# A gated recurrence and a highway layer: one product for e in most units, another order of the work, y in two tiles

## The chip, the cores and the metric

One core of a Trainium2 chip runs the whole kernel. The metric is the device time of one execution in microseconds, as the median of several runs. The profile shows one execution; its span, from the first to the last instruction, is shorter than the time of a run, which has some work around it.

## What is computed

x and f_logit have 4 sequences of 6336 steps with 256 channels each, in float32.

```python
sig = 1.0 / (1.0 + np.exp(-f_logit))
f = lower_bound[None, None, :] + (1.0 - lower_bound[None, None, :]) * sig
i = 1.0 - f
for t in range(S):
    h = f[:, t] * h + i[:, t] * x[:, t]
    y[:, t] = h
...
H = np.maximum(x @ w_h, 0.0)
T = 1.0 / (1.0 + np.exp(-(x @ w_t + b_t)))
return (T * H + (1.0 - T) * x).astype(np.float32)
```

In the last three lines, x is the y of the recurrence, as 25344 tokens of 256 channels.

## The kernel before, in words

The tokens are cut into 28 **units** (`parts`, line 42): units 0, 1 and 27 have 2 blocks of 128 tokens, units 2 and 26 have 4, all the others 8. The 256 channels are two halves of 128, so that in the middle of the kernel a channel lies on a partition and the tokens along the free dimension. Each unit goes through the same steps; a token of the list such as `s12.1:0` names the step, the unit, the half (or piece) and the buffer slot, and a `v` at its end gives the step to VectorE:

- **l**, **x**: loads of f_logit and x (SP's queue, line 244); 1 MB each for a unit of 8 blocks.
- **u** = sigmoid(-l) on ScalarE (line 256). **b** = u * x in pieces (line 264), on GpSimd or VectorE: for a unit of 8 blocks there are two pieces of 1024 elements a partition, b.0 and b.1, for the small units one or two of 512.
- **i**: PE transposes u half by half (line 271); **f** = 1 - c u from PSUM (lines 280 and 282), on ScalarE or VectorE. **p**: PE transposes pairs of b (line 291); it needs all pieces of b of its unit.
- **s**: the recurrence as one scan for each half (line 308) on VectorE, cut where a sequence begins; it reads f and the transposed b and writes y in bfloat16. A unit's scan starts from the last column of the scan before it, so the scans of a half form a chain.
- **z**, **g**: the two matrix products on PE (lines 320 and 114); **t** = sigmoid(z) on ScalarE (line 333); **d** = max(ncc y, g) on VectorE (line 337), where the weights have been changed so that this is relu less y in scaled form.
- **e**: d = d * t (line 343), on GpSimd or VectorE, in the pieces that the last entry of `units` gives (line 45).
- **o**: PE adds y and e and transposes them back (lines 365 and 366); **c** copies PSUM to SBUF (line 376 on VectorE, line 378 on ScalarE); **w** stores (line 382, SP's queue). o of a piece needs the e of its columns in both halves.
- **k** and `*n` put idle matmuls on PE (lines 125 and 114). Some tokens without a number are preparations: cc, dg, WT, WH, cb, pc, pb, and wt, wh for the weights' loads.

What sets the order: the list `order` (lines 48 to 98) is written out and read from its start to its end, and `tc.keep_in_program_order` keeps every engine's and every DMA queue's instructions in that order. So a step that waits holds everything behind it on its engine. Slots name buffers: a step that writes a slot waits until the readers of the slot's last contents are through. The waits between engines are put in by the tile framework.

One wait is put in by hand: `shared` (line 178). After VectorE has a product of two operands (b or e; also the preparations), the next such product on GpSimd in the list waits for it (only the next one, since the record is removed then). Nothing makes a product on VectorE wait for GpSimd. One line says it:

```python
tc.add_manual_dep(ins.ins, held.pop().ins.name, ...
```

y, d and t are each one tile for both halves of a unit (`flat`, line 296; `half` cuts the columns of one half out of it). y has four slots, d and t three each.

Of the kernel before, what the change touches and what calls it, by code (L numbers as in the profile page):

```python
# [12 lines left out]
BF16 = mybir.dt.bfloat16  # L13
# [6 lines left out]
def kernel(  # L20
# [53 lines left out]
p15.1:1 s15.1 c12.1:1 b17.1:2 f16.0:2 z14.1:0 z14.0:2 p16.0:0 s16.0:1 c12.0:3 t14.1:1 t14.0 g14.0:1 d14.0 i16.1:1
w11.1 l19:1 u18:3 x18:0 b17.0 e14.0 g15.1:0 d15.1:2 z15.0:2 i17.1:0 x19:3 f16.1:0 b18.0:3 p16.1:1 f17.1:1 b18.1 l20:2
s16.1 o13.1:1 t15.0:0 p17.0:0 g15.0:0 w12.1 d15.0 c13.1:0 u19:1 b19.1:1 o13.0:2 p17.1:1 z15.1:1 c13.0:2 z16.0:0
s17.1:2 t15.1 t16.0:1 z16.1:2 s17.0 g16.0:1 w13.1 t16.1 i18.0:1 d16.0:0 g16.1:0 o14.0:2 i18.1:0 f18.0:0 d16.1 e15.0v
o14.1:1 p18.0:1 s18.0:3 u20:2 w12.0 z17.0:0 c14.0:0 c14.1:1 f18.1:1 g17.0:2 d17.0:1 z17.1:1 b19.0 t17.0:0 i19.1:0
# [10 lines left out]
b25.1 p24.0:0 c20.1:1 d22.0 z23.0:0 s24.0:1 g23.0:1 t23.0:2 e22.0 l26:0 o21.0:2 c21.0:2 o21.1:0 s24.1 i25.1:0 g23.1:2
c21.1:3 x26:1 e22.2 g24.1:0 d23.0:1 f25.1:1 u26:2 b26.0:1 i27.1:1 i25.0:0 f27.1:0 d23.1 w20.0 z23.1:1 p25.0:1 f25.0:2  # L90
d24.1:2 s25.0:2 z24.0:2 p25.1:0 b26.1 t23.1 o22.0:0 e23.1 o22.1:1 t24.0:0 e23.2 z24.1:2 c22.0:0 s25.1 w20.1 g24.0:0
d24.0 e23.0v w21.0 c22.1:1 t24.1 w21.1 e24.0 w22.0 i26.0:1 e24.1 z25.0:1 i27.0:0 f26.0:2 g25.0:2 e24.2 i26.1:1 d25.0:0
f27.0:1 t25.0:1 p26.0:0 f26.1:3 o23.0:0 g25.1:1 z25.1:2 p26.1:1 s26.0:3 d25.1 c23.0:0 s26.1 w22.1 o23.1:0 p27.0:0
t25.1 w23.0 c23.1:1 o24.0:1 e25.0v o24.3:2 s27.0:0 g26.0:a1 o24.2:0 c24.0:2 o24.1:1 d26.0:1 c24.3:0 c24.2 c24.1
p27.1:0 e25.1 e25.2v z26.0:2 o25.0:0 o25.1:1 z26.1:a1 s27.1 g26.1:a0 t26.0:0 z27.0:2 c25.0:3 t26.1 c25.1v o25.2:0
t27.0:1 o25.3:1 d26.1 g27.0:a0 w23.1 z27.1:a1 w24.1 w24.0 e26.0 c25.2:0 e26.1v o26.0:2 o26.1:0 d27.0:0 g27.1:a0 d27.1
w25.0 c25.3 t27.1 e27.0 e27.1v o27.0:1 c27.0v:1 c26.0:2 o27.1:a0 c26.1 w25.1 w26.0 w27.0 c27.1:3 w27.1
"""

    NU = len(units)  # L100
# [7 lines left out]
    def sb(shape, dtype, name, slot=0):  # L108
        return pool.tile(shape, dtype, tag=f"{name}{slot}", name=name)
# [56 lines left out]
    def tokens(n):  # L166
        return units[n][0] * P
# [128 lines left out]
    def flat(n, key, name, slot):  # L296
        if key not in st[n]:
            st[n][key] = sb([P, NH * NB * P], BF16, name, slot)
        return st[n][key]

    def half(n, key, h):
        return st[n][key][:, h * tokens(n):(h + 1) * tokens(n)]

    def do_s(n, h, eng, slot):
        flat(n, "y", "y", slot)
        y = half(n, "y", h)
        for fresh, c, e in pieces(n):
            pin(nc.vector.tensor_tensor_scan(y[:, c:e], st[n]["f", h][:, c:e], st[n]["bT", h][:, c:e],  # L308
                                             0.0 if fresh else carry[h], op0=ALU.mult, op1=ALU.add))
            carry[h] = y[:, e - 1:e]  # L310
# [32 lines left out]
        shared(pin(e.tensor_mul(st[n]["d"][:, a:c], st[n]["d"][:, a:c], st[n]["t"][:, a:c])), not eng)  # L343
# [79 lines left out]
```

## Time and profile before

| | |
|---|---|
| median of 3 runs | 207.93 us (207.89 to 208.76) |
| span of the profiled execution | 206.1 us |
| instructions | 4635 |
| bytes moved | 78.68 MB, mean 382 GB/s |
| mean granted TensorE clock | 0.995 |

How to read it: PE is TensorE, PEld its weight loads, DVE VectorE, ACT ScalarE, POOL GpSimd, SP the queue that issues the DMAs. A row of a group gives line, engine, operation, what it writes from what it reads, the shape, the count, busy microseconds, the mean of one in nanoseconds, and the idle time just ahead of them with what ended it. A row of the timeline begins with start and duration in microseconds and may merge several instructions that follow each other (x2 and so on). Neighbours on an engine overlap a little, so that start to start is some 0.06 us less than the mean.

### The profile page before, as it was taken

How to read it: one execution, taken by the hardware profiler on the slowest of the kernel's cores; microseconds unless marked ns; L12 is line 12 of the kernel's file. 1: busy time of each engine (PE TensorE's matmuls, PEld its weight loads, DVE VectorE, ACT ScalarE, POOL GpSimd, SP SyncE). 2: the span in 40 equal slices, each digit the busy share in tenths (PEclk: the TensorE clock that was granted, in tenths of full speed). 3: DMA queues.
4: the chain of work that ended last, by engine and by line, in shares of the span. 5: the costliest groups of instructions: out<-in, count | busy, mean ns of one | idle time of the engine just before them, and what ended most of it. 6: DMA issues, size and time to landing. Idle time of an engine off the chain costs nothing.

```text
span 206.1 us, 4635 instructions
## 1 busy us (share of the span) xinstructions
PE 192.6 (93%) x1837; PEld 133.8 (65%) x1837; DVE 194.5 (94%) x159; ACT 191.9 (93%) x192; POOL 173.8 (84%) x93
## 2 busy tenths in 40 slices
PE   7798799799998999999999999999999999999991
PEld 2366465566685776676577576677758758776770
DVE  0899999999999999999899999999999999999972
ACT  4369999999999999999999999999999999999891
POOL 3036989789979997999999999799899999998840
PEclk9999999999999999999999999999999999999997
DMA  6999999999999999999999999999999999725396
GB/s 196 370 424 422 411 418 423 409 423 417 414 423 408 429 417 426 423 420 413 425 424 416 433 411 417 429 415 418 407 422 422 414 392 378 286 104 204 138 382 248
DMA packets 16125, 78.68 MB, mean 382 GB/s; under 512 B 1764, under 2 KB 2536, under 8 KB 10216
## 3 DMA queue, kind: packets, MB, share of 16 engines
q1 hardware_dynamic: 16096, 78.39, 93.6%
q8 instruction: 14, 0.23, 0.4%
q14 instruction: 7, 0.06, 0.1%
q10 hardware_dynamic: 8, 0.00, 0.0%
HBM read 52.43 MB, written 25.95 MB: 380 GB/s over the span
## 4 chain that ended last, share of the span: by engine, by line
PE 53%; ACT 14%; DMA 13%; DVE 10%; issue 6%; POOL 2%; SPq 1%; ACTq 0%; DVEq 0%; POOLq 0%
DMA x<-in_x_dram 9%; DVE y L308 8%; PE op L366 7%; PE bT L291 7%; PE op L365 7%; PE g L320 7%; PE z L320 6%; PE uT L271 6%; PE g L114 6%; PE z L114 6%; ACT o L378 4%; ACT f L282 4%; DMA out_dram<-o 4%; ACT t L333 3%; POOL bv L264 2%
## 5 line engine op out<-in xcount | busy, mean ns | idle before, releaser
L264 POOL TENSOR_TENSOR bv<-u,x 128x1024 bf16<-128x1024 f16 (+1 forms) x49 | 100.9, 2085 | 16.9 <-DVE bt L207 10.7
L308 DVE TENSOR_TENSOR_SCAN y<-f,y,bT 128x1024 bf16<-128x1024 f16 (+5 forms) x54 | 106.8, 1989 | 0.2 <-PE bT L291 0.2
L343 POOL TENSOR_TENSOR d<-d,t 128x512 bf16<-128x512 bf16 (+3 forms) x33 | 73.3, 2234 | 9.6 <-DVE d L343 4.2
L337 DVE SCALAR_TENSOR_TENSOR d<-y,ncc,g 128x1024 bf16<-128x1024 bf16 (+2 forms) x56 | 63.1, 1137 | 1.5 <-PE g L320 1.0
L333 ACT ACTIVATE t<-z,bt 128x1024 bf16<-128x1024 f32 (+2 forms) x56 | 58.9, 1088 | 1.3 <-PE z L114 0.7
L282 ACT ACTIVATE f<-uT,ncc 128x1024 f16<-128x1024 f16 (+2 forms) x51 | 55.4, 1098 | 3.4 <-PE uT L271 2.2
L378 ACT COPY o<-op 128x1024 f32<-128x1024 f32 (+2 forms) x55 | 52.1, 984 | 2.4 <-PE op L366 1.6
L256 ACT ACTIVATE u<-l 128x2048 f16<-128x2048 f32 (+2 forms) x28 | 49.8, 1781 | 2.8 <-DMA l<-in_f_logit_dram 2.7
L366 PE MATMUL op<-ident_b,d 128*128 128x128 bf16 x396 | 49.5, 219 | 0.6 <-DVE d L343 0.6
L365 PE MATMUL op<-diag,y 128*128 128x128 f16 x396 | 49.7, 219 | 0.1
L366 PEld LDWEIGHTS <-d 128*128 128x128 bf16 x396 | 44.0, 113 | 3.2 <-DVE d L343 0.7
L365 PEld LDWEIGHTS <-y 128*128 128x128 bf16 x396 | 44.2, 113 | 1.7
L320 PE MATMUL g<-y,w_sb 128*128 128x512 bf16 (+1 forms) x112 | 39.5, 367 | 0.9 <-DVE d L337 0.7
L320 PE MATMUL z<-y,w_sb 128*128 128x512 bf16 (+1 forms) x112 | 39.3, 367 | 0.4 <-ACT o L378 0.4
L291 PE MATMUL bT<-ident_f,bv 128*128 128x128 f32 x198 | 31.8, 277 | 4.3 <-DVE y L308 2.6
L114 PE MATMUL z<-y,w_sb 128*128 128x512 bf16 x92 | 34.9, 379 | 0.0
L114 PE MATMUL g<-y,w_sb 128*128 128x512 bf16 x92 | 34.9, 379 | 0.0
L320 PEld LDWEIGHTS <-w_sb 128*128 128x128 f16 x224 | 21.6, 98 | 17.5 <-issue 0.9
L271 PEld LDWEIGHTS <-u 128*128 128x128 f16 x396 | 26.3, 98 | 10.2 <-issue 2.6
L271 PE MATMUL uT<-ident_h,u 128*128 128x128 f16 x396 | 31.2, 220 | 1.6 <-DVE y L308 0.8
L291 PEld LDWEIGHTS bT<-ident_f,bv 128*128 128x128 f32 x198 | 22.4, 141 | 12.3 <-ACT f L282 3.0
L114 PEld LDWEIGHTS <-w_sb 128*128 128x128 f16 x184 | 18.0, 98 | 16.7 <-issue 1.8
(39 smaller groups left out, 58.7 us busy)
## 6 DMA issues: line engine op xcount, KB each, us to landing
out_dram<-o SPq DMA_DIRECT2D x48, 512.0 KB, 7.7
l<-in_f_logit_dram SPq DMA_DIRECT2D x23, 1024.0 KB, 12.0
x<-in_x_dram SPq DMA_DIRECT2D x23, 1024.0 KB, 13.4
l<-in_f_logit_dram SPq DMA_DIRECT2D x2, 512.0 KB, 7.5
x<-in_x_dram SPq DMA_DIRECT2D x2, 512.0 KB, 7.2
l<-in_f_logit_dram SPq DMA_DIRECT2D x3, 256.0 KB, 2.9
x<-in_x_dram SPq DMA_DIRECT2D x3, 256.0 KB, 3.9
out_dram<-o SPq DMA_DIRECT2D x2, 256.0 KB, 16.3
```

The lines of the kernel that those rows point to most:

```text
L114: return pe.add_instruction(mybir.InstMatmult(name=nc.get_next_instruction_name(), start_tensor_calc=start, stop_tensor_calc=stop, tile_si ...
L264: shared(pin(e.tensor_mul(st[n]["bv"][:, a:c].rearrange("p k d j -> p k j d"), st[n]["u"][:, 2 * a:2 * c].rearrange("p (k j) d -> p k j d" ...
L271: pin(nc.tensor.transpose(uT[:, j * P:(j + 1) * P], st[n]["u"][:, j, h * P:(h + 1) * P], ident_h))
L282: pin(nc.scalar.activation(to, of, AF.Identity, scale=ncc[:, h:h + 1], bias=1.0))
L291: pin(nc.tensor.transpose(words[:, k:k + g * (P - 1) + 1:g], pair, ident_f))
L308: pin(nc.vector.tensor_tensor_scan(y[:, c:e], st[n]["f", h][:, c:e], st[n]["bT", h][:, c:e], 0.0 if fresh else carry[h], op0=ALU.mult, op1 ...
L320: pin(nc.tensor.matmul(p[:, a:e], w, half(n, "y", ki)[:, a:e], start=ki == 0, stop=ki == NH - 1))
L333: pin(nc.scalar.activation(half(n, "t", m), st[n]["z", m][:, :tokens(n)], AF.Sigmoid, bias=bt[:, m:m + 1]))
L337: pin(nc.vector.scalar_tensor_tensor(half(n, "d", m), half(n, "y", m), ncc[:, m:m + 1], st[n]["g", m][:, :tokens(n)], op0=ALU.mult, op1=AL ...
L343: shared(pin(e.tensor_mul(st[n]["d"][:, a:c], st[n]["d"][:, a:c], st[n]["t"][:, a:c])), not eng)
L365: pin(nc.tensor.matmul(o, half(n, "y", h)[:, cols], diag[:, h], start=True, stop=False))
L366: pin(nc.tensor.matmul(o, half(n, "d", h)[:, cols], ident_b, start=False, stop=True))
```

## The change

Three things. The pieces of e: one product of 2048 elements a partition for units 3 to 25 (so far for units 7 to 21, the others of 8 blocks in three pieces of 1024, 512 and 512). y: a tile for each half, with eight slots of half the size, where there were four slots of a whole one; `half` takes the half's tile. The list: a new one, all of it in another order. The rest are other spellings of the same code.

On VectorE's queue the new list has b0, b1, b2.1, b2.0 and b26.0 (512 each) and b3.1, b4.1 (1024 each); before it was b0, b1, b2.1 and b3.1. Its e are now e0.0, e2.1, e6, e9, e15, e17, e25 and e27.1. It has copies c24.1, c25.3 and c26.0, where there were c25.1 and c27.0, and f1.0, f9.0, f10.0 and f18.0, where there were f0.0, f1.1, f9.0, f14.0 and f22.0. On SP's queue the loads of unit 0 stand first, wt is the third, and l27 and x27 stand in the middle of the queue instead of near its start. d24.1 stands behind the scan s25.0 instead of ahead of it. The diff, with the two lists cut to the lines that matter most:

```diff
     parts = [2] * 2 + [4] + [8] * 23 + [4] + [2]
+    bcuts = {2: (0, 1), 4: (0, 1, 2), 8: (0, 2, 4)}
+    ecuts = {2: (0, 256, 512), 4: (0, 512, 1024), 8: (0, 1024, 1536, 2048)}
     units, at = [], 0
     for n, nb in enumerate(parts):
-        units.append((nb, at, {2: (0, 1), 4: (0, 1, 2), 8: (0, 2, 4)}[nb], (0, 2048) if 7 <= n <= 21 else {2: (0, 256, 512), 4: (0, 512, 1024), 8: (0, 1024, 1536, 2048)}[nb]))
+        units.append((nb, at, bcuts[nb], (0, 2048) if 3 <= n <= 25 else ecuts[nb]))
         at += nb * P
...
-l1:0 l0:1 x0:0 x1:1 k*3:a0 l2:2 wt wh x2:2 l3:3 x3:3 l4:4 pc:0 x4:4 u0:0 l27:1 l5:5 b0.0v:0 x27:0 x5:5 u1:1 cc l6:0
...
-e8.0 t10.1:2 e9.0v b13.0:1 z10.0:0 f12.1:2 p11.1:1 b13.1 t10.0 o8.1:1 d10.1:0 p12.1:0 c8.1:0 o8.0:2 s11.1 u14:2
...
+l0:0 x0:0 u0:0 i0.1:0 pc:0 wt i0.0:1 l1:1 x1:1 wh l2:2 b0.0v:0 cc x2:2 f0.0:0 k*5:2 p0.0:1 WT f0.1:1 p0.1:0 s0.0:0 s0.1:1 dg
+u1:1 k*3:0 i1.1:1 z0.1:1 f1.1:2 l3:3 b1.0v:1 u2:2 z0.0:2 x3:3 i1.0:0 k*4:0 p1.1:1 f1.0v:3 pb:0 p1.0:0 WH cb s1.0:2 s1.1:3
...
+i8.0:0 g7.0:1 w3.0 x9:4 b9.0:1 b9.1 l10:5 b11.1:2 z7.0:2 f8.0:0 i9.1:1 i11.1:0 t7.0:1 f11.1:1 f9.1:3 g7.1:0 e6.0v w4.0 x10:5
...
+x26:5 g24.0:0 o22.0:1 d24.0 c22.1:2 w21.1 e23.0 g25.1:2 u26:3 c22.0:3 b26.1:0 d25.1:0 w21.0 i26.1:0 w19.0 b26.0v i26.0:1
...
     def half(n, key, h):
+        if key == "y":
+            return st[n][key, h][:, :tokens(n)]
         return st[n][key][:, h * tokens(n):(h + 1) * tokens(n)]
 
     def do_s(n, h, eng, slot):
-        flat(n, "y", "y", slot)
+        st[n]["y", h] = sb([P, NB * P], BF16, "y", slot)
         y = half(n, "y", h)
...
     def store(n):
-        return 1 if n in (27,) else 4
+        return 1 if n == 27 else 4
...
-        w = min(2 if n in (24, 25, 26,) else 4, store(n))
+        w = min(2 if n in (24, 25, 26) else 4, store(n))
```

More of the change, by code (lines that the diff above doesn't have):

```diff
@@ L74 @@
[L74 to L78, printed above, removed]
@@ L89 @@
[L89 to L93, printed above, removed]
@@ new lines @@
+f17.1:2 c13.0:2 l20:3 o13.1:0 s16.1:1 d15.1 p17.0:0 u19:0 x19:1 w13.0 z16.1:1 e14.0 i18.1:1 c13.1:1 s17.0:2 w13.1 g16.1:2
+d16.1:0 w11.0 z15.1:0 p17.1:0 t16.1:1 s17.1:3 x20:3 l21:4 g16.0:1 u27:1 f18.1:1 i19.1:1 b18.0:3 t15.1 b18.1 d16.0 z16.0:2
+b19.0:2 f19.1:3 t16.0 o14.0:0 e16.0 u20:3 b19.1 c14.0:2 w12.0 x21:4 i18.0:0 o14.1:1 p18.1:1 b20.0:0 e15.0v o15.1:2 f18.0v:0
+i19.0:0 g17.1:0 c14.1:1 s18.1:4 c15.1:3 z17.1:1 f19.0:2 p18.0:1 b20.1 t17.1:2 d17.1:2 z17.0:2 i20.1:0 t17.0 g17.0:0 s18.0:5
+o15.0:1 p19.1:1 w14.1 f20.1:1 u21:2 z18.1:2 p19.0:0 d17.0 t18.1:0 g18.1:0 c15.0:0 x27:5 w15.1 l22:5 w14.0 b21.0:1 b27.0:3
@@ new lines @@
+b23.1:0 b23.0 c19.1:2 i23.0:0 t21.0:0 o19.0:1 g21.0:0 f23.0:0 z21.1:2 p23.1:0 p23.0:1 w17.1 u24:2 l25:1 d21.0 e20.0 z22.0:0
+s23.1:6 c19.0:1 o20.0:1 t21.1 t22.0:1 z22.1:2 i24.0:0 g22.0:0 c20.0:3 s23.0:7 d22.0:0 g22.1:1 i27.0:1 x25:3 b24.0:1 b24.1
+t22.1 o20.1:2 g23.1:0 f24.0:3 i24.1:0 f27.0:2 d22.1 d23.1:2 u25:0 p24.0:1 f24.1:0 e21.0 w19.1 w20.0 w18.1 z23.0:1 z23.1:0
+c20.1:2 b25.0:2 b25.1 s24.0:0 p24.1:0 o21.1:2 w20.1 s24.1:1 t23.1:2 i25.0:1 g23.0:0 t23.0 e22.0 f25.0:3 o21.0:1 p25.0:1
+i25.1:0 c21.1:3 c21.0:0 d23.0 z24.0:2 t24.0:0 s25.0:2 f25.1:0 g24.1:0 z24.1:1 p25.1:1 d24.1:1 o22.1:2 s25.1:3 t24.1 l26:3
@@ L98 @@
+c26.1 e27.0 d27.1 e27.1v o27.0:1 c27.0:0 w26.0 o27.1:a1 w27.0 c27.1:1 w27.1
 """
```

68 lines of the change are left out of this document (31 added, 37 removed).

## The prediction

> **What bounds the kernel now.** I read the page's head first, then the table of stages, then who waited for whom on VectorE, then the prices by form, and last the order of time at the places that the new list touches.
>
> ```profile
> span 206.1 us, 4635 instructions
> PE 192.6 (93%) x1837; PEld 133.8 (65%) x1837; DVE 194.5 (94%) x159; ACT 191.9 (93%) x192; POOL 173.8 (84%) x93
> GB/s 196 370 424 422 411 418 423 409 423 417 414 423 408 429 417 426 423 420 413 425 424 416 433 411 417 429 415 418 407 422 422 414 392 378 286 104 204 138 382 248
> ```
>
> ```profile
> 0.00:20.33 20.33, 17.33 (x107) 9.47 (x108) 14.73 (x32) 12.70 (x17) 6.07 (x15) 1.00 0.93 351
> 20.33:182.81 162.48, 156.47 (x1520) 110.17 (x1519) 161.91 (x108) 161.72 (x151) 154.17 (x68) 1.00 1.00 409
> 182.81:206.10 23.29, 18.82 (x213) 14.14 (x211) 17.85 (x21) 17.48 (x26) 13.52 (x12) 0.96 0.55 215
> ```
>
> ```profile
> DVE bv L264 <- DMA x<-in_x_dram: 4.4, 1, 4.4
> DVE d L337 <- PE g L320: 1.0, 2, 0.8
> ```
>
> Four engines are near full, so shares alone decide nothing. In the table of stages (busy PE, weight loads, DVE, ACT, POOL; then granted clock, DMA share, GB/s) VectorE (DVE) is busy 161.91 of the middle 162.48 us: from unit 3's first scan at 20.33 to unit 25's first scan at 182.81 it never waits. It loses time only ahead of that (4.4 us for the first x) and in the last 23 us. GpSimd (POOL) is busy 154.17 of the same 162.48, so it has 8.3 us to spare; the DMA engines are full (share 1.00). VectorE sets the time, with GpSimd close behind. What is to be predicted is therefore VectorE's own work, and whether GpSimd still delivers in time.
>
> **Prices.** Mean ns of one, by form; neighbours on an engine overlap by 0.06 to 0.08 us, which I take off.
>
> ```profile
> L264 POOL TENSOR_TENSOR bv<-u,x 128x1024 bf16<-128x1024 f16 x45 | 96.2, 2165 | 5.4 <-DVE d L343 3.0 <-PE bT L291 1.3 <-DMA x<-in_x_dram 0.9
> L343 POOL TENSOR_TENSOR d<-d,t 128x2048 bf16<-128x2048 bf16 x12 | 49.1, 4096 | 0.1
> L264 POOL TENSOR_TENSOR bv<-u,x 128x512 bf16<-128x512 f16 x4 | 4.7, 1192 | 11.5 <-DVE bt L207 10.7 <-DVE d L343 0.8
> L308 DVE TENSOR_TENSOR_SCAN y<-f,y,bT 128x1024 bf16<-128x1024 f16 x40 | 92.8, 2334 | 0.2 <-PE bT L291 0.2
> L337 DVE SCALAR_TENSOR_TENSOR d<-y,ncc,g 128x1024 bf16<-128x1024 bf16 x46 | 57.4, 1258 | 0.4 <-issue 0.3
> L343 DVE TENSOR_TENSOR d<-d,t 128x2048 bf16<-128x2048 bf16 x3 | 3.9, 1295 | 0.0
> L343 DVE TENSOR_TENSOR d<-d,t 128x1024 bf16<-128x1024 bf16 x6 | 4.5, 756 | 0.0
> L343 DVE TENSOR_TENSOR d<-d,t 128x512 bf16<-128x512 bf16 x5 | 2.0, 420 | 0.1
> L264 DVE TENSOR_TENSOR bv<-u,x 128x512 bf16<-128x512 f16 x3 | 2.2, 721 | 4.4 <-DMA x<-in_x_dram 4.4
> L264 DVE TENSOR_TENSOR bv<-u,x 128x1024 bf16<-128x1024 f16 x1 | 1.8, 1753 | 0.0
> L280 DVE TENSOR_SCALAR f<-uT,ncc 128x256 f16<-128x256 f16 x2 | 1.0, 476 | 0.1
> L376 DVE COPY o<-op 128x512 f32<-128x512 f32 x1 | 0.7, 692 | 0.2 <-PE op L366 0.2
> ```
>
> Net: on GpSimd b 2.10, e of 2048 4.04, b of 512 1.13; on VectorE scan 2.25, d 1.19, e 1.22 / 0.69 / 0.35, b of 512 0.65, copy of 512 0.62.
>
> **VectorE up to unit 25's first scan.** In the built order of VectorE's queue, ahead of s25.0:
> - one d (d24.1) now stands behind it: -1.19;
> - its e products were three of 512, four of 1024 and three of 2048; they are one of 512 and four of 2048 (e6, e9, e15, e17): -2 x 0.35 - 4 x 0.69 + 1.22 = -2.24;
> - it takes b2.0 (512, 0.65) and b4.1 (1024) from GpSimd. The only 1024 that it did took 1.75 beside a GpSimd product; twice the 512 less its start is about 1.2. I take 1.2 (bounds 1.2 and 1.7): +1.85;
> - one f of 256 goes to ScalarE: -0.41.
>
> That is -2.0. Then the start:
>
> ```profile
> 4.12 1.15 ACT L256 ACTIVATE u<-l 128x512 f16<-128x512 f32 x2 [1.27 <-DMA l<-in_f_logit_dram]
> 5.52 0.73 DVE L264 TENSOR_TENSOR bv<-u,x 128x512 bf16<-128x512 f16 x1 [4.39 <-DMA x<-in_x_dram]
> 16.40 2.14 POOL L264 TENSOR_TENSOR bv<-u,x 128x1024 bf16<-128x1024 f16 x1 [0.72 <-DMA x<-in_x_dram]
> 17.96 1.75 DVE L264 TENSOR_TENSOR bv<-u,x 128x1024 bf16<-128x1024 f16 x1
> ```
>
> x0 was the third load and is now the second; the second (l0) released ScalarE at 4.12, so VectorE's first product starts near 4.2 instead of 5.52, 1.3 us sooner. Not all of it stays: the first scan waits for f0.0 and for five idle matmuls ahead of its transposes, and x3 (as many bytes ahead of it as before) still lands at about 16.4. Between 0 and 1.3 I keep 0.8. VectorE by itself would be at s25.0 at 182.81 - 2.0 - 0.8 = **180.0**.
>
> **GpSimd up to the same scan.** s25.0 needs both b of unit 25, now both on GpSimd.
>
> ```profile
> POOL d L343 <- DVE d L343: 4.2, 4, 1.6
> POOL bv L264 <- DVE d L343: 3.8, 4, 1.2
> ```
>
> ```profile
> 26.48 5.55 POOL L264 TENSOR_TENSOR bv<-u,x 128x512 bf16<-128x512 f16 x3 [0.84 <-DVE d L343]
> 131.26 2.15 POOL L264 TENSOR_TENSOR bv<-u,x 128x1024 bf16<-128x1024 f16 x1 [1.16 <-DVE d L343]
> 133.36 4.10 POOL L343 TENSOR_TENSOR d<-d,t 128x2048 bf16<-128x2048 bf16 x1
> 137.40 4.27 POOL L264 TENSOR_TENSOR bv<-u,x 128x1024 bf16<-128x1024 f16 x2
> 176.96 4.31 POOL L264 TENSOR_TENSOR bv<-u,x 128x1024 bf16<-128x1024 f16 x2
> 182.85 0.60 PE L291 MATMUL bT<-ident_f,bv 128*128 128x128 f32 x4
> ```
>
> Before, the row at 26.48 (b27.0 and, merged with it, two of 1024) ends at 32.03, so its last two (unit 5's pair, 4.27) began at 27.76, when x5 had landed. The 256 KB loads l27 and x27 no longer stand ahead of x5; 0.52 MB at the 424 GB/s of that slice is 1.24 us, so unit 5's b starts at 26.5. From there to the end of b25.1 the new queue has 42 b of 1024 (units 5 to 25), b27.0 and 15 e of 2048: 42 x 2.10 + 1.13 + 15 x 4.04 = 150.0, so 176.5. Four VectorE products (e6, e9, e15, e17) lie in between, and each holds GpSimd: the row at 131.26 shows 1.16 of idle while VectorE has one. Four of these are 4.6 (bounds 0, if GpSimd would have waited anyway, and 4 x 1.6, the longest of the eight of before). That gives 181.1 for b25.1, against 181.27 before, where the row at 176.96 ends. With the four transposes (0.60) and 0.1, s25.0 can start at **181.8**. So GpSimd, not VectorE, is late there: the 2.8 us that VectorE gains buy 1.0 us (182.81 to 181.8). What follows from SP's queue is no later: l25 and x25 have 1 MB less ahead of them than before, and though x9 has 2.5 MB more, it lands near 55 us by the sum of the slices, when GpSimd comes to it.
>
> **The last part.**
>
> ```profile
> 188.48 1.02 DVE L343 TENSOR_TENSOR d<-d,t 128x1024 bf16<-128x1024 bf16 x1
> 194.17 0.66 DVE L343 TENSOR_TENSOR d<-d,t 128x1024 bf16<-128x1024 bf16 x1
> 200.87 0.48 DVE L337 SCALAR_TENSOR_TENSOR d<-y,ncc,g 128x256 bf16<-128x256 bf16 x1 [0.78 <-PE g L320]
> 201.46 0.29 DVE L343 TENSOR_TENSOR d<-d,t 128x256 bf16<-128x256 bf16 x1
> 202.63 0.37 ACT L378 COPY o<-op 128x256 f32<-128x256 f32 x1 [1.30 <-PE op L366]
> ```
>
> From s25.0 to the end of the last product (e27.1, 201.75) before took 18.94. VectorE's work there: + d24.1 1.19, + b26.0 0.65 (was GpSimd's), e of two 1024 and two 512 (1.5 + 0.7 net) becomes one 2048 (1.22): -1.0; copies of 512 and 256 become three of 512: +0.95. Together +1.8. Its waits were 1.5 (the 0.78 above and smaller ones); with more work in the same place I take 1.0: b26.0 behind GpSimd's b26.1 about 0.5, its transposes 0.4, and little at the end. So 20.2, and e27.1 ends at 202.0, that is 0.3 later than before; from there to the end (o27.1, its copy, its store) nothing changes: 206.4.
>
> **Edits that I cost at nothing.** y in two tiles keeps eight halves, as many as four whole ones; a scan then waits for its own half of four units back, which was read long ago, and no such wait is among VectorE's. e in one product: o of units 3 to 6 and 22 to 25 waits for the whole 4.04 instead of a part; the copies and stores behind it are off the path until unit 25 (its e goes to VectorE at 1.22). If PE stood behind such an o, the next transposes, then a scan, would be late by up to 2 us. ScalarE does two copies of 512 less and one f of 256 more, PE fewer idle matmuls. The bytes are the same.
>
> **Sum.** -1.0 + 1.8 - 0.5 = +0.3 on 206.1. The runs' median is 207.93, 1.8 above the profiled span; I carry that over: **208.2**. A measurement of this kernel tells about 0.5% (1.04 us) from no change, so the forecast is no difference.
>
> **Rivals.**
> 1. GpSimd isn't late; VectorE's saving arrives. If the four holds fall where GpSimd would have waited for d or for a load, b25.1 ends near 176.5 plus little, and s25.0 starts at VectorE's 180.0: 206.1 - 2.8 + 1.8 - 0.5 = 204.6, with 1.8: 206.4. For it: GpSimd idled 8.3 us in the middle. Against: 8.0 us of GpSimd's idle were eight such holds, and they cost it as much there.
> 2. **The products meet.** Only GpSimd is made to wait, and only for products that stand ahead of it in the list; nothing makes VectorE wait.
>
> ```profile
> 129.76 1.42 DVE L343 TENSOR_TENSOR d<-d,t 128x2048 bf16<-128x2048 bf16 x1
> 125.81 4.29 POOL L264 TENSOR_TENSOR bv<-u,x 128x1024 bf16<-128x1024 f16 x2
> 186.65 2.30 POOL L343 TENSOR_TENSOR d<-d,t 128x512 bf16<-128x512 bf16 x2
> ```
>
> Here GpSimd's pair ends at 130.10; VectorE's e, begun 0.34 sooner, took 1.42, its sum less the overlap being 1.1; the 1024 at 188.48 took 1.02 against 0.66 (194.17) beside a product that ended at 188.95, and that at 17.96 was stretched likewise. So VectorE stands until GpSimd's product is through. In before all these overlaps are under 0.6 us. In the new list b9.0, b9.1 and b11.1 stand ahead of e6.0. VectorE comes to e6.0 at 20.3 + 11 x 2.25 + 8 x 1.19 + 0.35 + 1.2 = 56.1; GpSimd ends e5.0 at 26.5 + 8 x 2.10 + 3 x 4.04 = 55.4, and b9.0 waits for x9 until about then. Which is first can't be told; if GpSimd, VectorE stands for 2.1. The same holds at e15 and b19.0. Up to 1.8 us in all is covered by GpSimd's lateness; beyond it the end moves. Two such meetings, 4.2: s25.0 at 184.2, 2.4 later: **210.6**; that is the case on the slower side. The Trainium skill ("SBUF — State Buffer", section "Who interferes with whom") says that whichever of two such operations issues first has the shared pair of ports for its whole instruction and the other fully blocks; the trace agrees for VectorE's side (1.42), and no run here shows GpSimd's.
> 3. The change doesn't do what it says: y's halves and the single e free nothing, and only the order counts. It changes no number above.
>
> **Chances.** Forecast (GpSimd late by about as much as VectorE saves) 0.36; rival 1 0.33; rival 2 0.31. The range goes from 205.6 (rival 1 with all of the head's 1.3) to 210.6 (two meetings).
>
> **What will show it.** Head: VectorE's first product at 4.2, unit 3's first scan near 20.3. Middle: idle of VectorE ahead of scans, released by bT, would show GpSimd late; e of 2048 on VectorE longer than 1.3 us shows meetings. s25.0 at 181.8; 180 speaks for rival 1, 184 for rival 2. Tail: e27.1 ending 20.2 us after it. I'd be wrong if a load came later than its bytes say, or if PE stood behind an o and held up transposes.

## The result, and the profile after

The changed kernel takes **216.31 us** (median of 4 runs, 215.18 to 217.25) against 207.91 us of the kernel before beside it: 1.037 times as long, with a 95% interval of 1.031 to 1.044. The forecast was 208.2 us, the range 205.6 to 210.6. The profiled execution took 215.18 us, with a span of 213.4 us, 7.3 more than before.

The page of the kernel after, first the busy time:

```profile
span 213.4 us, 4563 instructions
PE 192.7 (90%) x1802; PEld 133.4 (63%) x1828; DVE 198.3 (93%) x154; ACT 192.4 (90%) x192; POOL 180.6 (85%) x82
GB/s 176 393 418 422 413 378 430 422 349 424 390 230 422 336 424 418 416 400 244 353 418 426 417 409 355 425 420 420 376 353 338 421 422 415 244 362 196 326 272 272
```

VectorE's two numbers hold the whole difference: it is busy 198.3 us instead of 194.5 (+3.8) and idle 213.4 - 198.3 = 15.1 us instead of 11.6 (+3.5). The DMA rate, which before stayed at 407 GB/s or more from the third slice to the 31st, now dips to 230 at 59 to 64 us, 244 at 96 to 101 us, and elsewhere. The table of stages (same columns as before, VectorE third), cut at unit 3's and unit 25's first scan, says where the idle time is:

```profile
0.00:21.47 21.47, 15.36 (x96) 8.79 (x98) 15.37 (x34) 14.15 (x20) 6.75 (x15) 1.00 0.92 353
21.47:188.36 166.89, 156.75 (x1494) 109.62 (x1514) 163.58 (x102) 159.75 (x148) 158.34 (x61) 1.00 0.98 383
188.36:213.40 25.04, 20.54 (x219) 14.96 (x219) 19.37 (x21) 18.51 (x26) 15.52 (x7) 0.99 0.72 285
```

Idle are 6.10, 3.31 and 5.67 us, before 5.60, 0.57 and 5.44. So 2.7 of the 3.5 us are in the middle, where VectorE hardly waited before.

**The busy time: meetings.** VectorE's five e of 2048 elements (time order):

```profile
58.21 2.85 DVE L344 TENSOR_TENSOR d<-d,t 128x2048 bf16<-128x2048 bf16 x1
88.68 1.53 DVE L344 TENSOR_TENSOR d<-d,t 128x2048 bf16<-128x2048 bf16 x1
133.84 1.82 DVE L344 TENSOR_TENSOR d<-d,t 128x2048 bf16<-128x2048 bf16 x1
146.66 2.44 DVE L344 TENSOR_TENSOR d<-d,t 128x2048 bf16<-128x2048 bf16 x1
202.97 1.22 DVE L344 TENSOR_TENSOR d<-d,t 128x2048 bf16<-128x2048 bf16 x1
```

The last is alone and takes 1.22. The other four, e6, e9, e15 and e17, take 8.64 where 4.88 would do: 3.76 us, all of the +3.8. And what GpSimd does at those four times (neighbours merged):

```profile
57.81 7.38 POOL L263 TENSOR_TENSOR bv<-u,x 128x1024 bf16<-128x1024 f16 x3
89.08 5.06 POOL L344 TENSOR_TENSOR d<-d,t 128x2048 bf16<-128x2048 bf16 x1
134.86 2.82 POOL L263 TENSOR_TENSOR bv<-u,x 128x1024 bf16<-128x1024 f16 x1 [0.28 <-DMA x<-in_x_dram]
143.76 7.35 POOL L263 TENSOR_TENSOR bv<-u,x 128x1024 bf16<-128x1024 f16 x3
```

Three b take some 6.35 us unhindered (6.34 in e4 below), one 2.16, and an e 4.08; here GpSimd is stretched by 1.0, 1.0, 0.7 and 1.0 us. So a meeting costs both: VectorE the rest of GpSimd's running product, GpSimd up to 1.0 us while VectorE's runs.

**The idle time: late inputs.** Who VectorE waited for between 21 and 189 us (the three largest rows, 2.4 of the 3.3 us), then GpSimd's queue at two places:

```profile
DVE y L309 <- issue: 0.9, 2, 0.7
DVE y L309 <- PE bT L290: 0.8, 2, 0.5
DVE y L309 <- PE uT L270: 0.7, 1, 0.7
```

```profile
27.98 2.16 POOL L263 TENSOR_TENSOR bv<-u,x 128x1024 bf16<-128x1024 f16 x1 [1.48 <-ACT u L255]
105.56 4.25 POOL L263 TENSOR_TENSOR bv<-u,x 128x1024 bf16<-128x1024 f16 x2 [3.14 <-DMA x<-in_x_dram]
```

Scans wait: 1.5 us for transposes (of b and of u), and 0.9 where the view names nothing that released them. The transposes of b wait for GpSimd, and the second of its rows shows one reason why it runs late: unit 15's b stood 3.14 us for its load x15. SP's queue, which issues loads and stores in one order, shows why that load was late:

```profile
87.46 0.97 SPq L383 DMA_DIRECT2D out_dram<-o  x2
88.48 0.78 SPq L243 DMA_DIRECT2D l<-in_f_logit_dram  x1
96.58 0.33 SPq L383 DMA_DIRECT2D out_dram<-o  x1
97.01 1.12 SPq L243 DMA_DIRECT2D x<-in_x_dram  x1
```

```profile
SPq L383 <- ACT o L379: 130.4, 32, 15.1
```

```profile
SPq L382 <- ACT o L378: 110.2, 37, 7.5
```

```profile
87.61 0.37 SPq L244 DMA_DIRECT2D x<-in_x_dram  x1
```

x15 is issued at 97.01, because the store w9.1 ahead of it waited for its copy until 96.58; for 7.3 us nothing was issued. Before (the last row) it was issued at 87.61. The two sums (after, then before) are the time that stores on the queue waited for ScalarE's copies: 20 us more, the longest twice as long.

### The profile page after: what moved, and what is told of

It reads as the page before. It is cut to its first block, busy times and chain, and to the rows that moved or that the text cites. A ratio compares the mean times of both kernels' runs of the same rounds, so it can differ in the third digit from the quotient of the medians.

```text
span 213.4 us, 4563 instructions
## 1 busy us (share of the span) xinstructions
PE 192.7 (90%) x1802; PEld 133.4 (63%) x1828; DVE 198.3 (93%) x154; ACT 192.4 (90%) x192; POOL 180.6 (85%) x82
## 4 chain that ended last, share of the span: by engine, by line
PE 44%; DVE 16%; ACT 10%; POOL 10%; issue 9%; DMA 7%; SPq 1%; POOLq 0%; ACTq 0%; DVEq 0%
DVE y L309 7%; PE op L367 6%; PE op L366 6%; PE g L321 6%; DMA x<-in_x_dram 6%; PE bT L290 5%; PE z L321 5%; POOL bv L263 5%; PE uT L270 5%; POOL d L344 5%; PE z L113 4%; PE g L113 4%; DVE d L338 3%; DVE d L344 3%; ACT t L334 3%
## 5 line engine op out<-in xcount | busy, mean ns | idle before, releaser
L263 POOL TENSOR_TENSOR bv<-u,x 128x1024 bf16<-128x1024 f16 (+1 forms) x46 | 98.9, 2176 | 22.1 <-ACT u L255 15.5
L344 POOL TENSOR_TENSOR d<-d,t 128x2048 bf16<-128x2048 bf16 (+2 forms) x25 | 81.6, 3268 | 5.5 <-DVE d L344 2.6
L334 ACT ACTIVATE t<-z,bt 128x1024 bf16<-128x1024 f32 (+2 forms) x56 | 56.4, 1037 | 3.0 <-PE z L113 1.5
L281 ACT ACTIVATE f<-uT,ncc 128x1024 f16<-128x1024 f16 (+2 forms) x52 | 53.4, 1042 | 6.0 <-PE uT L270 5.9
L379 ACT COPY o<-op 128x1024 f32<-128x1024 f32 (+2 forms) x54 | 49.3, 938 | 4.3 <-PE op L367 2.3
L255 ACT ACTIVATE u<-l 128x2048 f16<-128x2048 f32 (+2 forms) x28 | 48.4, 1732 | 3.2 <-DMA l<-in_f_logit_dram 3.2
L321 PE MATMUL g<-y,w_sb 128*128 128x512 bf16 (+1 forms) x110 | 38.7, 367 | 3.0 <-DVE d L338 1.2
L321 PE MATMUL z<-y,w_sb 128*128 128x512 bf16 (+1 forms) x109 | 38.6, 367 | 1.5 <-DVE y L309 0.7
L113 PE MATMUL z<-y,w_sb 128*128 128x512 bf16 x83 | 31.4, 379 | 0.1
L113 PE MATMUL g<-y,w_sb 128*128 128x512 bf16 x82 | 31.1, 379 | 0.1
```

What stands on the lines that cost most here:

```text
L113: return pe.add_instruction(mybir.InstMatmult(name=nc.get_next_instruction_name(), start_tensor_calc=start, stop_tensor_calc=stop, tile_si ...
L263: shared(pin(e.tensor_mul(st[n]["bv"][:, a:c].rearrange("p k d j -> p k j d"), st[n]["u"][:, 2 * a:2 * c].rearrange("p (k j) d -> p k j d" ...
L281: pin(nc.scalar.activation(to, of, AF.Identity, scale=ncc[:, h:h + 1], bias=1.0))
L321: pin(nc.tensor.matmul(p[:, a:e], w, half(n, "y", ki)[:, a:e], start=ki == 0, stop=ki == NH - 1))
L334: pin(nc.scalar.activation(half(n, "t", m), st[n]["z", m][:, :tokens(n)], AF.Sigmoid, bias=bt[:, m:m + 1]))
```

## The experiments

Theory 1, the meetings at the port; theory 2, loads that stand behind waiting stores; rivals: the single product of e itself, the halves of y, and the order on PE. The runs are numbered e1 to e18, like the products e of the units; where both could be meant, the text says run or product. Each run has its own runs of the kernel before on the same chip (medians 207.9 to 208.3). The kernel before repeats to within 1 us mostly; where products meet freely, executions of one kernel differ by several us, so for those the spread is given.

### Which part of the change: e1_old_order, e7_y_only, e2_y_whole, e3_e_pieces

```diff
 # e1: the list of before; e of units 3 to 6 and 22 to 25 whole, where the last piece stood, for example
-e6.0v ... e6.1 ... e6.2
+e6.0
 # e7: e1 with the pieces of before; e2: y in one tile again; e3: list after, e in three pieces
-(0, 2048) if 3 <= n <= 25
+(0, 2048) if 7 <= n <= 21
-e3.0
+e3.0 e3.1 e3.2
```

> The list of before with the other two parts of the change: y in two tiles, and e of units 3 to 6 and 22 to 25 in one product each, standing where the last piece stood. If the new list costs the time (meetings at the shared port, stores ahead of loads), this runs like the kernel before: 207 to 209.5 us, at most one or two overlaps of VectorE's e above 1.5 us, and no slice of the middle under 380 GB/s. If the single product or the halves of y cost it, it runs at 212 us or more.

> The list of before and its pieces of e, with y in two tiles as the only part of the change. The run with the old list and both other parts took 213.4 us, so this tells which of them cost its 5 us. If the single product of e did it: like the kernel before, 207.5 to 209 us. If the halves of y did it: 212 us or more.

> The kernel after with y in one tile for both halves again. If the halves of y are neutral, as forecast: 215 to 217.5 us. If the list needs them (a scan that no longer waits for the other half's readers): slower than after, 218 us or more. If they cost something: under 214 us.

> The kernel after, with e of units 3 to 6 and 22 to 25 cut into three pieces again, in the same place on the same engine. If the single product makes the copies and stores of these units late, and so the loads queued behind the stores, this gets back most of the 7 to 8 us (209 to 211 us) and the dip of the DMA rate at 59 to 64 us goes. If the list's order costs the time, it stays within 1 us of after (215 to 217.5 us), dips included.

| | e in pieces as before | e in one product |
|---|---|---|
| list before | 208.28 us (e7; 0.9996 times before, 0.9956 to 1.0036) | 213.38 us (e1; 1.026, 1.019 to 1.033) |
| list after | 222.66 us (e3; 1.071, 1.067 to 1.075) | 216.31 us (after) |

y is neutral on both sides: e7 is the kernel before, and e2 takes 215.45 us (1.031, 1.026 to 1.037), not to be told from after. But e1 was a miss: with whole products it takes 5 us more than e7 in the old list, and after takes 6 less than e3 in the new one. The two rows do not compare the same thing, though. e3 cuts each e in its place on its engine; e1 also moves work. Of the e whose pieces the two engines shared, e3, e6 and e23 are now wholly on GpSimd, e4, e5 and e25 wholly on VectorE, and each stands later than its first piece did. So e1 does not tell the length of the product from its place and its engine; no run did. VectorE in e1's profiled execution, the slowest of its four:

```profile
25.74 2.29 DVE L343 TENSOR_TENSOR d<-d,t 128x512 bf16<-128x512 bf16 x2
43.93 2.08 DVE L343 TENSOR_TENSOR d<-d,t 128x2048 bf16<-128x2048 bf16 x1
47.88 2.35 DVE L308 TENSOR_TENSOR_SCAN y<-f,y,bT 128x1024 bf16<-128x1024 f16 x1 [1.88 <-PE bT L289]
```

The two e of 512 take 2.29 here and 0.78 in before, but they stand ahead of the first e that was changed: the b beside them came late because GpSimd had waited 1.74 us for its load. Then the product e4, whole and on VectorE, meets one of GpSimd, and a scan waits; only these two come behind the edit. In run e3 the pieces of the product e6 stand at 58.56 for 7.37 us (VectorE, then GpSimd):

```profile
58.56 7.37 DVE L344 TENSOR_TENSOR d<-d,t 128x1024 bf16<-128x1024 bf16 x3
```

```profile
58.31 6.41 POOL L263 TENSOR_TENSOR bv<-u,x 128x1024 bf16<-128x1024 f16 x3
```

VectorE's first piece is 0.25 us later than GpSimd's first b and stands until the third has ended at 64.72. That is the place where it lost 1.6 us in after (2.85 for the whole): this one meeting is 4.5 us longer in run e3, of the 6.3 by which the run is slower than after.

### What a meeting is: e4_one_operand, e8_stt, e9_no_hold

```diff
 # e4 (units 6, 9, 15, 17; no hold)
-e.tensor_mul(d, d, t)
+nc.vector.tensor_scalar(d, d, ncc[:, :1], None, op0=ALU.mult)
 # e8 (the same units; no hold)
+nc.vector.scalar_tensor_tensor(d, d, 1.0, t, op0=ALU.mult, op1=ALU.mult)
 # e9: the kernel before, in shared
+        return
```

> The kernel after, with e of units 6, 9, 15 and 17 on VectorE multiplied by a constant of the channel in place of t (these four units leave t out of the result), so VectorE has no two-operand product there and holds nobody. Theory of the meetings: these four take 0.5 to 1.2 us each instead of 1.5 to 2.9, the GpSimd products beside them take 2.1 to 2.2 us again instead of 2.8 to 3.2, and the kernel gains the 4 to 6 us that VectorE gets back: 210 to 212.5 us. Theory of the late loads: VectorE gets the time back and then waits for loads; 214.5 to 216.5 us.

> The kernel after with e of units 6, 9, 15 and 17 as (d times 1.0) times t in the instruction that d uses, which no profile here shows stretched beside a GpSimd product; it holds nobody. If that form does not need the shared port: each takes 2.3 to 2.5 us whatever GpSimd does, GpSimd's products beside it take 2.17 us instead of 2.8 to 3.2, and e10 4.1 instead of 5.06. VectorE then stands about 1 us worse than after by these four, GpSimd 4 us better: 214 to 216 us if only VectorE counts, 211 to 213 us if GpSimd's lateness is what makes the scans wait. If the form needs the port too: stretched like after, 215 to 218 us.

> The kernel before without the hold: no GpSimd product waits for a VectorE product by hand any more; everything else as before. It prices meetings in the old list. If a meeting costs VectorE up to 1.7 us and GpSimd 1.0 us as in the profile after, several of VectorE's products stretch (the three of 2048 to 1.5 to 3 us, those of 1024 and 512 by up to 2 us) and the kernel is 2 to 6 us slower: 210 to 214 us. If GpSimd's 8 us of holds are what costs, it gets them back and the kernel is the same or up to 2 us faster: 206 to 208.5 us.

Neither other form escapes the port. The first of the four in e4 (whose profiled execution is its slowest, so that only lengths are read from it), with GpSimd beside it, and the same in e8:

```profile
58.24 5.87 DVE L344 TENSOR_SCALAR d<-d,ncc 128x2048 bf16<-128x2048 bf16 x1
```

```profile
57.21 6.34 POOL L263 TENSOR_TENSOR bv<-u,x 128x1024 bf16<-128x1024 f16 x3
```

```profile
58.40 3.57 DVE L344 SCALAR_TENSOR_TENSOR d<-d,t 128x2048 bf16<-128x2048 bf16 x1
```

With one operand VectorE stood through three GpSimd products and finished 0.56 us after the last (63.55). The other form took 3.57, against 2.28 for the shortest of its four. The d, which has one of its operands in PSUM, is never stretched (in e4 none took longer than 1.29 us). So neither run took the meetings away, and neither tells what the kernel is without them: e4 takes 214.58 us (213.08 to 219.73). e8 takes 220.88 us (219.55 to 233.29); its four take 12.25 us together, 3.6 more than in after, which is most of what it loses against after.

Without the hold the old list takes 219.5 to 237.7 us, at least 11 more; expected were 2 to 6. One of the meetings in its profiled execution (223.85 us), VectorE and GpSimd:

```profile
83.10 5.20 DVE L339 TENSOR_TENSOR d<-d,t 128x2048 bf16<-128x2048 bf16 x1
```

```profile
82.96 4.25 POOL L260 TENSOR_TENSOR bv<-u,x 128x1024 bf16<-128x1024 f16 x2
88.64 2.16 POOL L260 TENSOR_TENSOR bv<-u,x 128x1024 bf16<-128x1024 f16 x1 [1.43 <-ACT u L252]
```

VectorE waits not for the product that is running but for the end of both (87.21), and then needs its 1.1 us: 88.30. The Trainium skill ("SBUF — State Buffer", section "Who interferes with whom") says that whoever issues first has the shared pair for the whole instruction while the other fully blocks; these rows agree on the blocking, but here the second b, which began after VectorE's product had, went first too.

### Meetings away: e6_hold, e10_hold4, e11_left_out

```diff
 # e6: the hold falls on the product that was met (e15 also passes d16.0)
-b9.0:1 b9.1 l10:5 b11.1:2 ... g7.1:0 e6.0v
+e6.0v b9.0:1 b9.1 l10:5 b11.1:2 ... g7.1:0
-b18.1 d16.0 ... b20.0:0 e15.0v
+e15.0v b18.1 d16.0 ... b20.0:0
-b20.1 ... b21.0:1 b27.0:3 b21.1 s19.1:6 e17.0v
+... s19.1:6 e17.0v b20.1 b21.0:1 b27.0:3 b21.1
 # e10: e6, and
-e10.0 ... z11.1:2 e9.0v
+e9.0v e10.0 ... z11.1:2
 # e11: after, in do_e
+        if n in (6, 9, 15, 17):
+            return
```

> The kernel after with e6, e15 and e17 of VectorE placed in the list ahead of the GpSimd products that they met (e15 one d sooner on VectorE), so that the hold makes GpSimd wait and VectorE finds the port free; e9 is left. Theory of the meetings: the three take 1.2 us each instead of 2.85, 1.82 and 2.44, GpSimd idles 1 to 2 us at each, and as GpSimd has slack the kernel gains about 3 us: 212 to 213.5 us. Rival: VectorE gets the 3.5 us back, but GpSimd's later products come back as waits of the scans for their transposes, and the time stays at 215 to 217 us.

> The kernel with three held products, with the fourth (e9) placed ahead of e10 too, so that no GpSimd product that comes after it can take the port from it. In the run with three, e9 stood for 5.78 us, 4.6 more than unhindered, and the median was 218.2 us. Theory of the meetings: that part comes back, 213 to 214.5 us, which is 2 us better than after. Rival (what VectorE does not lose at the port GpSimd loses at the hold, and the scans wait for it): 215.5 us or more.

> The kernel after without e of units 6, 9, 15 and 17: these four units leave out the product with t. VectorE loses 4 times 1.14 = 4.6 us of work and all four meetings (3.6 us), GpSimd the 3.6 us by which its products were stretched. If the rest of the loss (waits of the scans, 3.7 us) comes from GpSimd's stretched products too: under 206 us. If only work and meetings go: 207 to 209 us. If loads and the order of the list set the time, whatever VectorE does: 211 us or more.

e6 takes 218.23 us (216.59 to 220.71; the profiled one is the slowest). The three held products take 1.20 each, but the product e9, which was left free, is caught (VectorE, GpSimd):

```profile
89.59 5.78 DVE L343 TENSOR_TENSOR d<-d,t 128x2048 bf16<-128x2048 bf16 x1
```

```profile
86.01 4.26 POOL L262 TENSOR_TENSOR bv<-u,x 128x1024 bf16<-128x1024 f16 x2
90.23 4.06 POOL L343 TENSOR_TENSOR d<-d,t 128x2048 bf16<-128x2048 bf16 x1
```

With all four held (run e10) the product e9 takes 1.65 and the others 1.20, so that 0.4 us of the meetings is left, and the time is 216.60 us, as after. The holds have their own price. GpSimd is busy 3.5 us less, but waits 9.7 us for VectorE's e (4.1 in after):

```profile
POOL bv L262 <- DVE d L343: 5.8, 3, 2.3
POOL d L343 <- DVE d L343: 3.9, 2, 2.6
```

So run e10 takes the meetings from VectorE and charges GpSimd for them. Leaving the four products out altogether (run e11) has neither meetings nor holds there, and gives 215.26 us: VectorE's meetings alone do not explain the loss. The pages of e10 and e11:

```profile
PE 193.4 (90%) x1828; PEld 133.8 (62%) x1828; DVE 196.1 (91%) x154; ACT 192.4 (90%) x192; POOL 177.1 (82%) x82
```

```profile
PE 194.0 (91%) x1828; PEld 133.3 (62%) x1828; DVE 192.0 (90%) x150; ACT 192.1 (90%) x192; POOL 177.0 (83%) x82
```

In e10 VectorE is busy 2.2 us less than after and idle 214.9 - 196.1 = 18.8 us, 3.7 more; in e11 busy 6.3 less, and idle 213.9 - 192.0 = 21.9 us, 6.8 more. Who GpSimd and ScalarE wait for in e11:

```profile
POOL bv L263 <- DMA x<-in_x_dram: 8.5, 6, 3.3
```

```profile
ACT u L255 <- DMA l<-in_f_logit_dram: 4.2, 6, 1.0
```

In after these are 4.0 and 3.2. With less to do on VectorE, the others stand longer for the loads: a second wall close behind the first.

### Loads: e5_loads_first, e12_x15_first

```diff
 # e5: 32 stores of units below 20 moved behind up to two loads, for example
-w4.0 x10:5 ... w2.0 w4.1 l12:0 ... w5.0 x12:0
+x10:5 ... l12:0 w4.0 ... x12:0 w2.0 w4.1 ... w5.0
 # e12
-w9.1 x15:4
+x15:4 w9.1
```

> The kernel after, with 32 stores of units below 20 moved behind up to the next two loads on SP's queue. Theory of the late loads: the dips of the DMA rate at 59 to 64 and 96 to 101 us go (over 380 GB/s there), GpSimd's 3.1 us wait for x15 at 105 us goes, and the kernel gains 3 to 4 us: 212 to 213.5 us. Theory of the meetings: the loads are earlier, but VectorE stands as long as before at its four products; 215 to 217 us.

> The kernel after with the load x15 and the store w9.1 exchanged on SP's queue, nothing else. GpSimd's 3.1 us wait for x15 near 105 us should be gone or under 1 us. If GpSimd's lateness there is what later makes the scans of units 16 to 19 wait: 1 to 2 us faster than after (214 to 215 us). If it is absorbed, or shifts GpSimd into other meetings: 215.5 to 218 us.

e5 fills the first dips (423 GB/s at 59 to 64 us) and takes 216.48 us all the same: the stores are now late, ScalarE's copies wait 5.3 us for their slots, and the rate falls to 236 at 91 to 96 us. e12 removes the 3.14 us at unit 15's b entirely and takes 214.88 us (1.029, 1.023 to 1.036), 1.4 less than after, though the intervals overlap.

### Loads that stand behind nothing: e13_free_stores, e14_free_hold4, e15_free_left_out, e16_free_before

```diff
+    const = sb([P, 4, D], FP32, "const")
+    nc.gpsimd.memset(const, 0.0)
...
-st[n]["o", j0][:, :j1 - j0]
+const[:, :j1 - j0]
```

> The kernel after with every store reading one constant tile in place of the copies (the copies are still made; what is stored is not the result). The bytes, the queue and its order are the same, but no store waits for a copy any more, and so no load stands behind such a store. Theory of the late loads: no slice of the middle under 390 GB/s, GpSimd's and ScalarE's waits for loads (4.0 and 3.2 us) gone, and with them at least half of the 8 us: 208 to 212 us. If the loads don't matter: 214 to 217 us.

> The same stores of a constant, in the kernel with the four held products (216.6 us without it, though VectorE lost almost nothing at the port). Theory that both count, one behind the other: 207 to 210 us, less than with the free stores alone. If the meetings never mattered: like the free stores alone, or slower by GpSimd's holds.

> The same stores of a constant, in the kernel without e of units 6, 9, 15 and 17 (215.3 us without it, where GpSimd waited 8.5 us for loads of x and ScalarE 4.2 us for f_logit). If the late loads are the wall that took up the 8 us which VectorE had gained there: 203 to 207 us. If it is another wall (the order on PE): 210 us or more.

> Control: the same stores of a constant in the kernel before, whose DMA rate is already above 400 GB/s up to 160 us. Theory of the late loads: within 1 us of the kernel before (207 to 209 us). If waiting stores cost the old list as much as the new one, it is 2 us or more faster.

| | real stores | stores that wait for nothing | difference |
|---|---|---|---|
| before | 208.05 us | 205.85 us (e16; 0.990, 0.988 to 0.993) | -2.2 |
| after | 216.31 us | 218.8 to 225.6 us (e13) | slower |
| after, four holds | 216.60 us (e10) | 211.79 us (e14; 1.019, 1.017 to 1.021) | -4.8 |
| after, four products left out | 215.26 us (e11) | 205.88 us (e15; 0.990, 0.988 to 0.992) | -9.4 |

The control's 2.2 us are the end of the kernel, where the last store no longer waits for its copy (e27.1 ends at 202.0 us there, at 201.75 in before). Beyond them the edit is worth 2.6 us with the holds and 7.2 us without the four products: that is the second wall. It frees more than the loads: copies no longer wait for a store to leave their slot (ScalarE waited 3.6 us for that in e10, 2.6 in e11), and no run tells the two apart. And e13, the miss, shows the first one bare (VectorE, then GpSimd):

```profile
130.73 11.30 DVE L346 TENSOR_TENSOR d<-d,t 128x2048 bf16<-128x2048 bf16 x1
```

```profile
128.43 4.33 POOL L265 TENSOR_TENSOR bv<-u,x 128x1024 bf16<-128x1024 f16 x2
132.67 4.09 POOL L346 TENSOR_TENSOR d<-d,t 128x2048 bf16<-128x2048 bf16 x1
136.68 4.27 POOL L265 TENSOR_TENSOR bv<-u,x 128x1024 bf16<-128x1024 f16 x2
142.10 2.17 POOL L265 TENSOR_TENSOR bv<-u,x 128x1024 bf16<-128x1024 f16 x1 [1.16 <-DVE d L346]
```

With every load there in time GpSimd has no gap, and the product e15 stands through the second, third, fourth and fifth of these products (10.2 us), until the next is held for it by hand. PE runs dry meanwhile (busy 0.92 of the 7 us from 136 to 143), and its granted clock is 0.50 in that stretch. In after, the product e15 came in at GpSimd's 0.28 us wait for a load ahead of 134.86. It looks as if the late loads kept this meeting short; in any case, mending them alone made the kernel slower.

e14 has both walls away, at the price of the holds, and is still 5.9 us over e16, 1.3 of it busy time of VectorE (195.6 against 194.3) and 4.9 idle (14.4 against 9.5). Two of its waits:

```profile
142.43 2.35 DVE L310 TENSOR_TENSOR_SCAN y<-f,y,bT 128x1024 bf16<-128x1024 f16 x1 [1.29 <-ACT u L256]
168.29 1.28 DVE L339 SCALAR_TENSOR_TENSOR d<-y,ncc,g 128x1024 bf16<-128x1024 bf16 x1 [1.44 <-PE g L112]
```

The first is 0.69 in after (its scan at 144.40), the second is not in after, nor in run e18 below, which lacks the hold of the product e17. With 0.7 us each at two places where after waits too (42.18, and 198.13 for the transposes of unit 26) they are 4.1 us that e16 has not. Of these the whole second wait and 0.6 of the first are not in after, so some 2 us came in with the holds. The others are waits behind PE and ScalarE, whose order the new list sets; no run changed that order by itself. Run e15, without these holds, is level with run e16, but 4.9 us of VectorE's work are left out of it: its VectorE is idle for 13.6 us, against 9.5.

### Both with real stores: e17_both, e18_both3

```diff
 # e17: the four holds of e10, and loads ahead of the store that held them, in eight places
-w4.0 x10:5
+x10:5 w4.0
-w12.1 b17.1 x18:0 ... l20:3 ... x19:1
+x18:0 l20:3 x19:1 w12.1 b17.1
 # e18: the same without the hold of e17.0v
```

> The four holds (216.6 us alone), and eleven loads (x10, x12, x14, x15, x18, l20, x19, l23, x23, l24, x24, l26, x26 in eight places) placed ahead of the store that they stood behind on SP's queue; x15 alone without holds gave 214.9 us. Real stores, the reference's result. Theory of two walls, one behind the other: the two together give more than each alone, 211.5 to 214 us. If late loads only trade places with late copies, as in the run with 32 stores moved: 215 to 217 us.

> The same with three holds: e17 of VectorE is left to meet GpSimd's product, since its hold made later scans and d wait for 1.4 and 1.5 us in the run with four. Two walls: 211 to 214 us, better than with four holds by up to 2 us, if e17 loses no more than the 1.2 us of the profile after; up to 10 us worse if GpSimd has no gap there and e17 stands as long as e15 did with the free stores (11.3 us).

Both missed: 220.80 us (1.063, 1.058 to 1.069) and 220.24 us. One stall decides. In run e17, ScalarE and VectorE:

```profile
130.75 1.01 ACT L378 COPY o<-op 128x1024 f32<-128x1024 f32 x1 [4.61 <-DMA out_dram<-o]
```

```profile
134.62 2.35 DVE L308 TENSOR_TENSOR_SCAN y<-f,y,bT 128x1024 bf16<-128x1024 f16 x1 [5.96 <-PE bT L289]
```

w12.1 now goes behind 3 MB of loads; the next copy into its slot waits 4.6 us, PE 4.9 for that copy, and the scan 6.0. The same stall is in run e18. The expectation had the rival right: on one queue late loads trade places with late copies. That the hold of the product e17 costs about what it saves is all that the pair tells of it (220.8 against 220.2).

## Why the prediction was wrong, point by point

Two steps of the sum failed. It has no term for VectorE standing behind GpSimd's products (measured: 3.76 us); it charged four holds to GpSimd instead. And it took every load to be no later than its bytes say, so that nothing stands in it for stores that wait ahead of a load (measured: x15 was issued 9.4 us later than before, and GpSimd waited 4.0 us for loads).

- **What bounds the kernel: half right.** VectorE did carry the difference, busy and idle. But "the DMA engines are full" was noted and then dropped: a resource at share 1.00 that gets nothing new to do until a copy is made is a wall too.
- **"What follows from SP's queue is no later": failed.** It counted bytes ahead of a load, not the waits of the stores ahead of it. x15 was issued 9.4 us later than before, and GpSimd stood 3.1 us for it.
- **GpSimd "181.1" for b25.1: it was 187.6.** The start was 27.98, not 26.5, since unit 5's b waited for u5 on ScalarE, not for x5 (+1.5); the four holds of 4.6 were instead 3.7 of stretched products (-0.9); loads cost 4.0; the rest are small waits. Still, s25.0 at 188.36 followed directly on VectorE's own d, and the last of its transposes, which follow b25.1, had ended at 188.12:

```profile
187.45 0.67 PE L290 MATMUL bT<-ident_f,bv 128*128 128x128 f32 x4
```

So GpSimd was not what was last there, but by 0.24 us only: both were late by nearly the same, and a quicker VectorE alone could have gained no more at this scan, unless GpSimd gained with it. The forecast's "GpSimd is late" was seen only earlier, as short waits of scans.

- **VectorE's work: right.** -2.0 and +1.8 make -0.2; without the 3.76 of the meetings its busy time is the same as before (198.3 - 3.8 = 194.5).
- **The head: wrong by 1.2.** VectorE's first product came at 4.25 as forecast (4.2), but the first scan of unit 3 at 21.47, not 20.3. The row below shows where the gain went, the wait for wt, now the third load; besides, e0.0 and one d of unit 2 more stand between 16.6 us and that scan (0.9 more than in before).

```profile
6.48 0.61 DVE L216 TENSOR_SCALAR w_sb<-w_raw,cc 128x256 f16<-128x256 f32 x2 [1.39 <-DMA w_raw<-in_moe_w_t_dram]
```

- **Rival 2: the right mechanism, at two of its four places, too small.** It named e6 with b9.0, and e15. It held 1.8 us for covered and two meetings for enough: 210.6. There were four (3.8 us), and nothing covered them. Its price, the rest of one GpSimd product, is only the lower case: runs show 5.2, 5.8, 6.7 and 11.3 us. The list showed the other two as well: e9 and e17 also stand behind GpSimd products that nothing holds.
- **y at nothing: right** (0.9996). **The single e at nothing, or up to 2 us: wrong.** In the new list it saves 6.3 us (e3), most of it at one meeting, and by the timing that it happens to give. What it costs by itself in the old list stays open, since e1's 5.1 us hold a change of place and engine too.
- **The last part: right.** From s25.0 to the end of e27.1 20.9 us (forecast 20.2); b26.0's transposes cost 0.67 instead of 0.4.
- **The doubt at the end** ("if a load came later than its bytes say") was the right one, and it had no chance of its own among the cases.

What is shown: meetings without a hold cost VectorE and GpSimd time (e9, e13, and rows of every run); the waits that real stores bring, of loads and of copies, are a second wall (e14 against e10, e15 against e11, with the control). Neither mended alone gains more than 1.4 us. With both away (e14 against e16) some 2.5 of the 8.4 us go and 5.9 stay. What stays open is that rest: some 2 us of it came in with the holds, and the rows place most of the others behind PE and ScalarE; no run isolates them.

## What to carry to other kernels

On a queue with stores in it, a load's time is not bytes over rate: look which store stands ahead of it and when that one's copy is made. Where two engines share a port and only one is made to wait, price a collision by how long the other can run without a gap, not by one of its instructions, and ask for each unprotected product who else is there. In an order written out by hand, the parts of a change need not add up: price them together, and if freeing one engine gains nothing, look at what its neighbours then wait for.

## What the runs showed of the hardware that had not been expected

- A VectorE product can stand through four GpSimd products that follow each other (11.30 us in e13), of which three began after it; in after, e6 came in between two (2.85). What decides between these was not found.
- Operations that stand like that on VectorE: tensor_tensor with both operands in SBUF, tensor_scalar with one (5.87 against 1.38 at its shortest; the f of 1024 elements, the same operation from PSUM, took 1.25 to 1.27), scalar_tensor_tensor with two (3.57 against 2.28). The scans and the d, with one operand in PSUM, were never stretched.
- GpSimd is blocked in its turn: in after an e of 4.08 took 5.06, and the longest b, otherwise 2.16, took 3.17.
